# Top-k attention and a low-rank mixer: masking of the tails moves from VectorE to ScalarE and GpSimd

## The chip, the cores and the metric

One core of a Trainium2 chip runs the whole kernel. The metric is the device time of one execution in microseconds (us). Names of the engines in the profile: PE is TensorE (PEld its weight loads), DVE is VectorE, ACT is ScalarE, POOL is GpSimd, SP is SyncE, which issues most of the DMA transfers. The engines run side by side; each takes its own instructions strictly in the order in which the program issues them, and waits at an instruction until its inputs are ready and its output buffer is free.

## What is computed

Two blocks follow each other, all in float32:

```python
# attention: q, k, v are (8 batches, 8 heads, 576 rows, 64)
scores = scale * np.matmul(q, k.transpose(0, 1, 3, 2))
kth = np.partition(scores, -32, axis=-1)[..., -32:-32 + 1]
scores = np.where(scores >= kth, scores, -1000000000.0)
attn = softmax(scores)                    # exp, then divided by (sum + 1e-9)
x = np.matmul(attn, v)                    # then heads side by side: (8, 576, 512)

# mixer: U (576, 32), V (32, 576), w_ch1 (512, 2048), w_ch2 (2048, 512)
h = x.transpose(0, 2, 1) @ U @ V
u = x + h.transpose(0, 2, 1)
out = u + np.maximum(u @ w_ch1, 0.0) @ w_ch2
```

For every row of scores only the 32 largest of 576 take part in the softmax. U, V and the two large weights come as float64 and are converted on the chip, in pieces, while the attention of the first batches runs.

## The kernel before

**Pairs and steps.** The attention is done for pairs of heads: pair g (0 to 31) holds two heads of one batch, four pairs to a batch. A pair takes five steps. Steps t = 0 to 3 treat 128 rows of each head: two chunks of 128 x 576 scores, chunk 0 for the first head, chunk 1 for the second. Step t = 4 is the tail: the last 64 rows of both heads, stacked into one chunk of 128 x 576. Steps are numbered n = 5 g + t.

**One step** (`front`). `scores` has put the chunks into SBUF (Ssb, copied from PSUM by ACT one step ahead). VectorE finds the 8 largest of each row (L339, `first`), then three times replaces the 8 found by a very low number (L351) and finds the next 8 (L355). The last of the 32 is the row's threshold. A chunk is then masked and its exponential taken in one of three ways:

- *early*: ACT takes the exponential of the whole chunk soon after the first maximum is known (L348, `weigh`, L312); after the last maximum VectorE multiplies it by "score is at least the threshold" and sums the row (L361, `scalar_tensor_tensor`; the sum needs a short second instruction).
- *pooled* (chunk 1 of full steps): POOL computes a very low number where the score lies below the threshold (L358) and adds it to the scores (L359); ACT then takes the exponential with the row's sum.
- *gap* (chunk 0 of the steps for which `eased` is true): ACT forms `least`, the threshold times 2^96 (L375), and Relu of 2^96 times how far the score lies below the threshold (L376); POOL subtracts that from the scores (L377); ACT then takes the exponential with the sum (L381).

Before the change, full steps of the first two batches (g < 8) take *pooled* and *gap*. The exception is step 3 of pair 3, the last full step of the first batch: both its chunks are *early*. All tails are *early*. From the third batch on, full steps take *early* and *pooled*.

**After the mask.** `turns` transposes the exponentials on TensorE (L397, L402) and ACT copies them out of PSUM (PT, L398, L403); `values` multiplies them with v (L421, L431, L434); `mixed` scales by the reciprocal of the row sums (`inverse`, L409 and L410 on VectorE; L460 on POOL), and adds the low-rank part (L466 to L488). When all four pairs of a batch are through, its MLP (`mlp`, matmuls L503 and L522, ACT's Relu L515, POOL's add L538) becomes a list of fillers, which `fill` takes up in portions between the instructions of the next batch's attention. So the first batch has no MLP work beside it, and from then on there is always some.

**Order.** The order of each engine is written out by hand in the loop over n: `front(n)`, `turns` and the others are generators, and each `next(...)` issues one piece. `here` is the front of this step, `last` that of the step before. If the step before was eased, its gap piece is issued at the start of this step (in the batches after the first too) and its exponentials after that; in the first batch the exponentials come after the second `next(here)`. Steps 19 and 20 (the tail of pair 3 and the first step of pair 4), where the first batch ends, have a branch of their own (L612 to L643). `next_params` issues the float64 conversion: ACT L165 to L168, VectorE L175, POOL L176 and L178.

**Buffers.** Ssb and E have three buffers each, the transposes' PSUM tile two, PT two.

Of the kernel before, what the change touches and what calls it, by code (L numbers as in the profile page):

```python
# [11 lines left out]
AF = mybir.ActivationFunctionType  # L12
ALU = mybir.AluOpType

TOPK = 32
NEG = -3.0e38
# [4 lines left out]
WIDEN = 2.0**96  # L21
# [5 lines left out]
def kernel(  # L27
# [28 lines left out]
    nc = tc.nc  # L56
# [6 lines left out]
    NT, TAIL = 4, 64  # L63
# [3 lines left out]
    NPAIR = H // 2  # L67
# [243 lines left out]

        nc.scalar.activation(E, chunk, AF.Exp, bias=nmax, scale=SCALE, accum_out=total)  # L312

    def eased(g, t):


        return g < 2 * NPAIR and t < NT and (g, t) != (NPAIR - 1, NT - 1)

    def front(g, t):

        if t == 0:
            dens[g] = small.tile([P, 2 * NT + 1], F32, tag="den", name="den", bufs=3)
        chunks, den = S2s.pop((g, t)), dens[g]
        n = len(chunks)
        E2 = attn.tile([P, 2 * S], F32, tag="E", name="E", bufs=3)
        Es = [E2[:, c * S : (c + 1) * S] for c in range(n)]  # L330
        sums = [den[:, 2 * t + c : 2 * t + c + 1] for c in range(n)]
        probs[g, t] = E2
        curs, ms = list(chunks), [None] * n
        first = small.tile([P, 2, 8], F32, tag="first", name="first", bufs=3)
        nmax = small.tile([P, 2], F32, tag="nmax", name="nmax", bufs=4)
        order = (1, 0) if n == 2 else (0,)
        for c in order:
            ms[c] = first[:, c]
            nc.vector.max(ms[c], curs[c])  # L339
        yield  # L340
        ease = eased(g, t)
        pooled = n == 2 and (g, t) != (NPAIR - 1, NT - 1)
        early = range(0 if ease else 1 if pooled else n)
        for i in range(1, TOPK // 8):
            if i == 1:
                nc.scalar.mul(nmax[:, 0:n], first[:, 0:n, 0], -SCALE)
                for c in early:
                    weigh(chunks[c], Es[c], nmax[:, c : c + 1])  # L348
            for c in order:
                nxt = attn.tile([P, S], F32, tag="rr", name="rr", bufs=3)  # L350
                nc.vector.match_replace(nxt, ms[c], curs[c], NEG)  # L351
                curs[c] = nxt
            for c in order:
                ms[c] = small.tile([P, 8], F32, tag="m8", name="m8", bufs=8)
                nc.vector.max(ms[c], curs[c])  # L355
            yield
        if pooled:
            nc.gpsimd.tensor_scalar(Es[1], chunks[1], ms[1][:, 7:8], NEG, ALU.is_lt, ALU.mult)  # L358
            nc.gpsimd.tensor_tensor(chunks[1], chunks[1], Es[1], ALU.add)  # L359
        for c in early:  # L360
            nc.vector.scalar_tensor_tensor(  # L361
                out=Es[c],
                in0=chunks[c],
                scalar=ms[c][:, 7:8],
                in1=Es[c],
                op0=ALU.is_ge,
                op1=ALU.mult,
                accum_out=sums[c],
            )
        if t == NT:  # L370
            del qkTs[g]
        yield
        if ease:
            least = small.tile([P, 1], F32, tag="least", name="least", bufs=3)
            nc.scalar.mul(least, ms[0][:, 7:8], WIDEN)  # L375
            nc.scalar.activation(Es[0], chunks[0], AF.Relu, bias=least, scale=-WIDEN)  # L376
            nc.gpsimd.tensor_tensor(chunks[0], chunks[0], Es[0], ALU.subtract)  # L377
            yield
        for c in order:
            if c not in early:  # L380
                weigh(chunks[c], Es[c], nmax[:, c : c + 1], sums[c])  # L381
        if t == NT and g != NPAIR - 1:
            nc.scalar.activation(den, den, AF.Identity, bias=eps)
        yield
# [27 lines left out]
    def values(g, t):  # L412

        PT = PTs.pop((g, t))
        va, vd, vt = (a[g % NV] for a in (vas, vds, vts))
        O = ps_t.tile([P, P], F32, tag="tp", name="O")
        if t == NT:
            den, x = dens[g], xs[g % 2]
            inverse(g, 2 * NT if g == NPAIR - 1 else 0, 2 * NT + 1)
            for j in range(NT + 1):  # L420
                nc.tensor.matmul(  # L421
                    O,
                    lhsT=PT[:, j],
                    rhs=va[:, :, j, :] if j < NT else vt,
                    start=(j == 0),
                    stop=(j == NT),
                )
            for h in range(2):
                nc.scalar.mul(x[half(h), NT, half(h)], O[half(h), half(h)], den[half(h), 2 * NT :])
            return  # L430
        nc.tensor.matmul(O, lhsT=vd, rhs=PT[:, 2 * NT], start=True, stop=False)  # L431
        for j in range(NT):
            for h in range(2):
                nc.tensor.matmul(  # L434
                    O[half(h)],
                    lhsT=va[:, h, j, :],
                    rhs=PT[:, NT * h + j],
                    start=False,
                    stop=(j == NT - 1),
                )  # L440
        if t == 0:
            XTs[g] = attn.tile([P, MAIN], F32, tag="XT", name="XT")
        nc.scalar.copy(XTs[g][:, cols(t)], O)  # L443
# [152 lines left out]
    t = 0  # L596
# [5 lines left out]
    for n in range(STEPS + 2):  # L602
        g, t = divmod(n, CH)
        if n < STEPS:
            if t == 0 and g + 1 < NP:
                load(g + 1)
            if t == 1 and g + 1 < NP:
                ready = prep(g + 1)
            fronts[n] = front(g, t)
            next(fronts[n])  # L610
        here, last = fronts.get(n, iter(())), fronts.pop(n - 1, iter(()))
        if n >= ALONE - 1 and n <= ALONE:  # L612

            if n < ALONE:
                values(*divmod(n - 3, CH))
                list(turning)
                scores(*divmod(n + 1, CH))
                values(*divmod(n - 2, CH))
                next(here)
            list(turns(*divmod(n - 1, CH)))  # L620
            values(*divmod(n - 1, CH))
            if n < ALONE:
                inverse(g, 0, 2 * NT)
                next(here)
                mixing.append(mixed(g, 1))
                fill()
                next(here)
                next(here)
                continue
            fill()  # L630
            scores(*divmod(n + 1, CH))
            next(here)
            while mixing:
                fill()
            next_params(1)
            fill()
            next(last, None)
            next(here)
            fill()
            next(here)  # L640
            next(here)
            fill()
            continue  # L643
        ease = eased(*divmod(n - 1, CH))
        if n < ALONE:
            if ease:
                next(last, None)
            scores(*divmod(n + 1, CH))
            if n >= 3:
                values(*divmod(n - 3, CH))  # L650
                if (n - 3) % CH == NT:
                    mixing.append(mixed((n - 3) // CH, 3))
            list(turning)
            fill()
            next(here)
            if t < NT:
                next_params(1)
            fill()
            next(ready, None)
            next(here)  # L660
            next(last, None)
            fill()
            next(here)
            if t in (0, 1):
                next_params(1)
            next(here)
            fill()
            if n >= 1:
                turning = turns(*divmod(n - 1, CH))
            continue  # L670
        if ease:
            next(last, None)
        fill()
        next(turning, None)
        fill()
        next(turning, None)
        fill()
        next(ready, None)
        fill()
        if ease:  # L680
            next(last, None)
        if n - 2 >= ALONE:
            values(*divmod(n - 2, CH))
        if n + 1 < STEPS:
            scores(*divmod(n + 1, CH))
        next(here, None)
        next_params(1)
        if n - 2 >= ALONE and (n - 2) % CH == NT:
            mixing.append(mixed((n - 2) // CH, 4))
        fill()  # L690
        next(here, None)
        fill()
        if n <= STEPS:
            turning = turns(*divmod(n - 1, CH))
        next(turning, None)
        fill()
        next(here, None)
        next(last, None)
        if t in (1, 3):
            next_params(1)  # L700
        next(here, None)
        fill()
# [33 lines left out]
```

## Time and profile before

| what | us |
|---|---|
| median of five runs | 1850.42 |
| the five runs | 1848.48, 1848.49, 1850.42, 1850.67, 1850.97 |
| the profiled execution, time | 1848.48 |
| its span in the trace | 1846.7 |
| VectorE L361, 130 instructions, mean of one with its read | 0.89 |
| ACT L376, 31 instructions, mean | 0.776 |
| POOL L377, 31 instructions, median | 1.412 |
| POOL L358 and L359, mean | 2.236 and 1.409 |

The profile is of one execution. It gives for every instruction its start and length and, where its engine stood idle before it, which instruction ended the wait. A line such as "PE tp L397 <- ACT E L312" means that TensorE's transpose of line 397 waited for the exponential of line 312. The granted clock is the share of TensorE's full clock that it was given.

### The profile page before, as it was taken

The numbers are of one execution on the slowest core, as the hardware profiler recorded it, in microseconds if no ns is written. First come the engines' busy times: TensorE is split into PE (matmuls) and PEld (weight loads), VectorE is DVE, ScalarE is ACT, GpSimd is POOL, SyncE is SP. The second block draws the span as 40 slices with busy tenths as digits, with TensorE's granted clock in tenths as the row PEclk, the third lists the DMA queues.
The fourth block names the chain that finished last, engine by engine and source line by source line (L and its number), as shares of the span: only waits on it lengthen the run. The fifth ranks groups of instructions, "written<-read, shape, count | busy, mean of one in ns | idle before, by whom it ended". The sixth has DMA issues, their size and how long they took to land.

```text
span 1846.7 us, 29134 instructions
## 1 busy us (share of the span) xinstructions
PE 1740.1 (94%) x10528; PEld 1317.0 (71%) x10528; DVE 1575.9 (85%) x3224; ACT 1008.2 (55%) x2494; POOL 672.6 (36%) x463
## 2 busy tenths in 40 slices
PE   4666889999999999999999999999999999999999
PEld 2444556787777877787777877788777877778677
DVE  7999988998999999998999999999999999996000
ACT  5777777665645555555555555555555556454110
POOL 4677577443333323423223332323224333332000
PEclk7678899999999999999999999999999999999999
DMA  4232221101001010111000010110001010000000
GB/s 109 77 85 84 69 77 47 31 21 32 20 22 28 15 27 20 31 25 31 15 25 20 23 30 21 30 24 24 17 19 31 21 32 19 10 8 7 6 15 12
DMA packets 127295, 58.22 MB, mean 32 GB/s; under 512 B 89904, under 2 KB 124976, under 8 KB 127152
## 3 DMA queue, kind: packets, MB, share of 16 engines
q1 hardware_dynamic: 126096, 56.10, 11.4%
q8 instruction: 84, 1.38, 0.3%
q14 instruction: 59, 0.48, 0.1%
q10 hardware_dynamic: 1056, 0.26, 0.1%
HBM read 46.89 MB, written 9.44 MB: 31 GB/s over the span
## 4 chain that ended last, share of the span: by engine, by line
PE 84%; DVE 9%; POOL 3%; ACT 2%; issue 1%; DMA 0%; SPq 0%; POOLq 0%; DVEq 0%; ACTq 0%
PE mm L503 26%; PE mm L522 26%; PE sc L294 7%; PE O L434 6%; PE tp L397 6%; DVE rr L351 4%; DVE m L355 3%; PE sc L281 2%; PE O L421 2%; PE up L478 2%; PE O L431 1%; DVE first L339 1%; PE tp L266 1%; PE tp L550 1%; PE up L480 1%
## 5 line engine op out<-in xcount | busy, mean ns | idle before, releaser
L355 DVE MAX8 m<-rr 128x8 f32<-128x576 f32 x864 | 614.7, 748 | 5.5
L522 PE MATMUL mm<-hT,w 128*128 128x256 f32 (+1 forms) x2048 | 563.8, 411 | 0.0
L503 PE MATMUL mm<-uT,w 128*128 128x256 f32 (+1 forms) x2048 | 557.0, 410 | 1.6 <-ACT hT L515 1.6
L358 POOL TENSOR_SCALAR E<-Ssb,m 128x576 f32<-128x576 f32 x127 | 284.0, 2236 | 584.4 <-DVE m L355 398.3
L503 PEld LDWEIGHTS mm<-uT,w 128*128 128x128 f32 x2048 | 363.5, 190 | 107.9 <-issue 27.6
L522 PEld LDWEIGHTS mm<-hT,w 128*128 128x128 f32 x2048 | 361.4, 191 | 98.2 <-issue 23.3
L351 DVE MATCH_REPLACE8 rr<-m,rr 128x576 f32<-128x576 f32 x576 | 427.6, 742 | 0.0
L398 ACT COPY PT<-tp 128x512 f32<-128x512 f32 x288 | 168.4, 587 | 128.8 <-PE tp L397 127.9
L312 ACT ACTIVATE E<-Ssb,nmax 128x576 f32<-128x576 f32 x288 | 222.8, 776 | 24.4 <-POOL Ssb L359 14.2
L351 DVE MATCH_REPLACE8 rr<-first,Ssb 128x576 f32<-128x576 f32 x288 | 211.7, 741 | 0.0
L397 PE MATMUL tp<-ident,E 128*128 128x128 f32 x1152 | 179.2, 280 | 31.7 <-ACT E L312 13.4
L339 DVE MAX8 first<-Ssb 128x8 f32<-128x576 f32 x288 | 205.0, 748 | 1.5 <-ACT Ssb L307 1.5
L397 PEld LDWEIGHTS tp<-ident,E 128*128 128x128 f32 x1152 | 142.6, 144 | 82.4 <-ACT E L312 22.9
L361 DVE SCALAR_TENSOR_TENSOR E<-Ssb,m,E 128x576 f32<-128x576 f32 x130 | 115.7, 890 | 90.4 <-ACT E L312 78.0
L359 POOL TENSOR_TENSOR Ssb<-Ssb,E 128x576 f32<-128x576 f32 x127 | 179.0, 1409 | 10.6
L294 PE MATMUL sc<-qkT 64*128 64x288 f32 x1024 | 169.3, 451 | 11.7 <-ACT Ssb L305 7.7
L515 ACT ACTIVATE hT<-mm 128x320 f32<-128x320 f32 (+1 forms) x256 | 104.2, 407 | 119.1 <-PE mm L503 118.7
L434 PE MATMUL O<-PT,va 128*64 128x128 f32 x2048 | 143.0, 283 | 0.0
L443 ACT COPY XT<-O 128x128 f32<-128x128 f32 x128 | 34.2, 267 | 182.2 <-PE O L434 182.2
L294 PEld LDWEIGHTS sc<-qkT 64*128 64x128 f32 x1024 | 92.3, 196 | 50.2 <-issue 16.5
L538 POOL TENSOR_TENSOR oT<-oT,uT 128x320 f32<-128x320 f32 (+1 forms) x56 | 44.6, 796 | 224.5 <-ACT oT L537 224.5
L434 PEld LDWEIGHTS O<-PT,va 128*64 128x64 f32 x2048 | 111.7, 139 | 15.9 <-issue 0.9
(80 smaller groups left out, 1533.4 us busy)
## 6 DMA issues: line engine op xcount, KB each, us to landing
raw<-in_moe_w_ch_dram SPq DMA_DIRECT2D x32, 512.0 KB, 3.7
va<-in_v_dram SPq DMA_DIRECT2D x64, 128.0 KB, 2.4
out_dram<-ob SPq DMA_DIRECT2D x64, 128.0 KB, 1.9
ld_q<-in_q_dram SPq DMA_DIRECT2D x63, 128.0 KB, 2.7
ld_k<-in_k_dram SPq DMA_DIRECT2D x63, 128.0 KB, 2.7
ld_ends<-in_q_dram SPq DMA_DIRECT2D x32, 32.0 KB, 2.1
ld_ends<-in_k_dram SPq DMA_DIRECT2D x32, 32.0 KB, 2.1
vd<-in_v_dram SPq DMA_DIRECT2D x64, 16.0 KB, 2.0
```

What stands on the lines that cost most here:

```text
L294: nc.tensor.matmul(sc[:, h, 0:HALF], lhsT=qkT[half(h), 0, cols(t)], rhs=qkT[half(h), 1, i * HALF : (i + 1) * HALF], start=True, stop=True,)
L312: nc.scalar.activation(E, chunk, AF.Exp, bias=nmax, scale=SCALE, accum_out=total)
L339: nc.vector.max(ms[c], curs[c])
L351: nc.vector.match_replace(nxt, ms[c], curs[c], NEG)
L355: nc.vector.max(ms[c], curs[c])
L358: nc.gpsimd.tensor_scalar(Es[1], chunks[1], ms[1][:, 7:8], NEG, ALU.is_lt, ALU.mult)
L359: nc.gpsimd.tensor_tensor(chunks[1], chunks[1], Es[1], ALU.add)
L397: nc.tensor.transpose(tp[:, j, :], E2[:, a : a + P], ident)
L398: nc.scalar.copy(PT[:, NT * h : NT * h + NT], tp)
L434: nc.tensor.matmul(O[half(h)], lhsT=va[:, h, j, :], rhs=PT[:, NT * h + j], start=False, stop=(j == NT - 1),)
L503: nc.tensor.matmul(ph[:, 0:w], lhsT=w1[:, cc, f * P : (f + 1) * P], rhs=uT[:, cc, lo:hi], start=(cc == 0), stop=(cc == NC - 1),)
L522: nc.tensor.matmul(po[:, 0:w], lhsT=w2[:, f, c * P : (c + 1) * P], rhs=hTs[f][:, 0:w], start=(f == 0), stop=(f == NF - 1),)
```

## The change

A new function `ways` says for each step which chunks are *early*, *pooled* and *gap*, and `eased` follows from it. Two groups of chunks change their way:

- the tails of the first two batches, except that of pair 3 (pairs 0, 1, 2, 4, 5, 6, 7): from *early* to *gap*;
- chunk 1 of step 3 of pair 3: from *early* to *gap*.

Since `eased` is now true for these steps, their gap piece and their exponential are issued in the step after. In the branch of step 19 two `next(last)` are added for the second group, and the `next(here)` that issues the tail's first round (ACT's nmax and exponential among it) now comes before the copies of the next scores. A step's small addition of 1e-9 to the sums (L383) follows the tail's exponential.

```diff
+    def ways(g, t):
+        if g < 2 * NPAIR and (g, t) != (NPAIR - 1, NT):
+            if (g, t) == (NPAIR - 1, NT - 1):
+                return (0,), (), (1,)
+            return (), (1,) if t < NT else (), (0,)
+        return (0,), (1,) if t < NT else (), ()
+
     def eased(g, t):
-        return g < 2 * NPAIR and t < NT and (g, t) != (NPAIR - 1, NT - 1)
+        return bool(ways(g, t)[2])
...
-        ease = eased(g, t)
-        pooled = n == 2 and (g, t) != (NPAIR - 1, NT - 1)
-        early = range(0 if ease else 1 if pooled else n)
+        early, pooled, gaps = ways(g, t)
...
-        if pooled:
-            nc.gpsimd.tensor_scalar(Es[1], chunks[1], ms[1][:, 7:8], NEG, ALU.is_lt, ALU.mult)
-            nc.gpsimd.tensor_tensor(chunks[1], chunks[1], Es[1], ALU.add)
+        for c in pooled:
+            nc.gpsimd.tensor_scalar(Es[c], chunks[c], ms[c][:, 7:8], NEG, ALU.is_lt, ALU.mult)
+            nc.gpsimd.tensor_tensor(chunks[c], chunks[c], Es[c], ALU.add)
...
-        if ease:
+        for c in gaps:
             least = small.tile([P, 1], F32, tag="least", name="least", bufs=3)
-            nc.scalar.mul(least, ms[0][:, 7:8], WIDEN)
-            nc.scalar.activation(Es[0], chunks[0], AF.Relu, bias=least, scale=-WIDEN)
-            nc.gpsimd.tensor_tensor(chunks[0], chunks[0], Es[0], ALU.subtract)
+            nc.scalar.mul(least, ms[c][:, 7:8], WIDEN)
+            nc.scalar.activation(Es[c], chunks[c], AF.Relu, bias=least, scale=-WIDEN)
+            nc.gpsimd.tensor_tensor(chunks[c], chunks[c], Es[c], ALU.subtract)
             yield
...
             if n < ALONE:
+                next(last)
                 values(*divmod(n - 3, CH))
                 list(turning)
+                next(here)
+                next(last)
                 scores(*divmod(n + 1, CH))
                 values(*divmod(n - 2, CH))
-                next(here)
             list(turns(*divmod(n - 1, CH)))
```

## The prediction

> **What bounds the kernel now.** I read the page's engine sums and forty slices first, then a table of busy time by stage, then the waits of VectorE and TensorE, and last the timeline at three places: a tail, the border of the two first batches, and the first tail of batch 1.
>
> The page, sums and slices (a digit is a slice of 46.2 us):
>
> ```profile
> PE 1740.1 (94%) x10528; PEld 1317.0 (71%) x10528; DVE 1575.9 (85%) x3224; ACT 1008.2 (55%) x2494; POOL 672.6 (36%) x463
> PE   4666889999999999999999999999999999999999
> DVE  7999988998999999998999999999999999996000
> ```
>
> The sums say TensorE. The slices say that this is an average over two kernels: up to some 200 us VectorE is full and TensorE half idle. The table by stage (length; busy PE, PEld, DVE, ACT, POOL; granted clock; DMA):
>
> ```profile
> 11.00:218.40 207.40, 127.19 (x792) 84.47 (x789) 204.21 (x421) 148.23 (x355) 136.33 (x100) 0.75 0.29 82
> 218.40:318.00 99.60, 89.54 (x523) 62.47 (x522) 89.06 (x178) 75.93 (x179) 73.55 (x51) 1.00 0.23 70
> 318.00:1691.00 1373.00, 1367.59 (x8527) 1047.91 (x8526) 1277.24 (x2612) 756.83 (x1894) 457.29 (x293) 1.00 0.09 23
> ```
>
> Until 218.4, where the first MLP matmul starts, VectorE is busy 204.21 of 207.40 us: it sets the time. From 318 on TensorE is busy 1367.59 of 1373.00: nothing saved on VectorE counts there, and the end is the moment of 318 plus fixed matmul work. Between lies a mixed stage: TensorE idles 10.06 us of 99.60, in waits that lead back to VectorE, through POOL and ACT. So the question is by how much the change moves the moment of 318. TensorE's order of instructions is the same in both kernels.
>
> The waits up to 320 us (who waits, on whom: us in total, times, the longest), first VectorE's, then TensorE's from 205 us on:
>
> ```profile
> DVE E L361 <- ACT E L312: 11.1, 3, 5.9
> ...
> PE tp L397 <- ACT E L312: 3.3, 2, 2.0
> PE pT L466 <- POOL x L460: 1.7, 1, 1.7
> ```
>
> VectorE's only wait of weight in this stretch is L361's own; TensorE's longest are for exponentials and for POOL.
>
> The timeline of VectorE at the tail of pair 0 (start, length), at the tail of pair 4, and of TensorE at 317.6:
>
> ```profile
> 58.04 0.76 DVE L355 MAX8 m<-rr 128x8 f32<-128x576 f32 x1
> 58.94 0.82 DVE L361 SCALAR_TENSOR_TENSOR E<-Ssb,m,E 128x576 f32<-128x576 f32 x1
> 59.68 1.42 DVE L339 MAX8 first<-Ssb 128x8 f32<-128x576 f32 x2
> ...
> 258.40 0.76 DVE L355 MAX8 m<-rr 128x8 f32<-128x576 f32 x1
> 264.05 0.82 DVE L361 SCALAR_TENSOR_TENSOR E<-Ssb,m,E 128x576 f32<-128x576 f32 x1 [4.89 <-ACT E L312]
> 264.80 1.42 DVE L339 MAX8 first<-Ssb 128x8 f32<-128x576 f32 x2
> ...
> 317.61 0.88 PE L397 MATMUL tp<-ident,E 128*128 128x128 f32 x4 [1.95 <-ACT E L312]
> 318.28 3.29 PE L522 MATMUL mm<-hT,w 128*128 128x320 f32 x6
> ```
>
> The masking multiply (L361) sits between a tail's last maximum and the next pair's first one. At pair 4 it also makes VectorE stand 4.89 us for an exponential.
>
> **The change, part by part.**
>
> *Tails of pairs 0, 1, 2 (batch 0).* VectorE loses one L361 each. From the start of the last maximum to the next pair's first maximum are 59.68 - 58.04 = 1.64 us; two maxima back to back start 1.41 - 0.74 = 0.67 apart. So 0.97 us each (107.26 to 108.90 and 156.48 to 158.12 give the same), 3 x 0.97 = 2.91. VectorE is full here, the next scores lie ready 4 us before (their last copy ends at 153.85 for the maximum at 158.12), so all of it counts. Instead ACT gets least and Relu (L375 0.20, L376 0.78), an accumulator read (0.19), and the exponential later; POOL a subtraction (L377, 1.41). All this falls in step t = 0 of the next pair, where ACT has an idle stretch of 2.3 to 3.5 us before its next least and POOL one of 6.6 before the parameter join at 64.28, 113.49, 162.71. The transposes that read the result come a step later. Cost 0. If that cover were gone, the scores copies behind the Relu would slip by 1 us; their reader is 8 us away. No DMA or queue of SP is moved.
>
> *Second head of pair 3's step 3.* One of two L361 goes: 202.40 - 201.66 = 0.74 saved. But its sum now comes from ACT, and VectorE's den add (L409, 204.79) follows it in the middle of the tail's four maxima. Walk ACT, in the clock of before: the early exponential of this head is gone from the pair at 196.63, so the queue runs 0.68 ahead and ends the pair's earlier exponentials at 201.1 instead of 201.8. Least and Relu to 202.05; POOL, idle from 198.9 on, subtracts to 203.5. TensorE's transposes start 0.68 sooner (201.92 to 201.24); their three copies end at 203.95; then nmax (0.2), the tail's exponential (0.7), the head's exponential and sum (1.0): 205.85. So L409 starts at 205.9, not 204.79: +1.1 where -0.74 was to be had. Behind it stand the tail's remaining two rounds; the 0.29 that VectorE waits at 208.61 goes (that exponential is now early), and the first maximum of pair 4 starts at 210.18 instead of 209.35: **+0.83**. TensorE, meanwhile, gains: the copies of PT at 208.48 waited behind the tail's exponential, which now lies before them, so its chain to the first MLP matmul ends about 1.0 earlier. The wait is bounded by 0 (VectorE -0.74) and by the longest that VectorE now waits for L312, 5.9 at 319.80 (then about +5.2). I take +0.83 since it is added up from rows within 15 us of the place.
>
> *Tails of pairs 4 to 7 (batch 1).* At pair 4 VectorE no longer stands for the exponential; it waits for the scores instead, whose last copy (262.82, 0.28) ends at 263.10: 264.80 - 263.10 = **1.70** saved. Does TensorE follow? Its waits from 262 to 299 are 0.76 at 266.41 (a PT copy, which comes 0.7 earlier as ACT's exponential at 263.24 leaves the queue), 1.73 at 286.16 (POOL's x, three steps from VectorE) and 0.51: 2.5 to 3.0 of slack for 1.7, so yes. From 286.47 to 316.7 POOL is nearly full and leads to 317.61; its start hangs on VectorE's shift (285.74), its restart at 299.36 on TensorE's matmul before 298.85, and both move alike. The bounds: 0 if TensorE or ACT keeps the old pace, 1.70. I take 1.70. Tails 5, 6 and 7 lie at 318 and later: TensorE's stage, 0 (if TensorE no longer covered them, another 0.97 saved each). Their 1.41 of POOL falls into its idle 12.59 and 14.34 us (before 330.07 and 380.51).
>
> Sum: -2.91 + 0.83 - 1.70 = **-3.78 us** at 318, and so at the end. Profiled execution: span 1846.7, time 1848.48, which gives 1844.7. It is the lowest of the five (two at 1848.48 and 1848.49, three from 1850.42 to 1850.97), 1.94 below the median; on the median, 1850.42 - 3.78 = **1846.6**.
>
> *The clock.* After the 1.95 us idle before 317.61 four transposes took 0.88 (at 309.64: 0.60) and six matmuls 3.29 (at 308.02: 1.78): 1.8 us lost, with 0.58 granted from 318 to 322. A stretch of that kind may go or another come as idle stretches shift: 1.8 either way, kept for the range. The Trainium skill, TensorE: Matmul & The Clock Gate, HAM oscillation, warns only of idle gaps above some 3.4 us. The trace lowers the clock after less. By the page nothing would be at stake here and the sum stays -3.78; the row decides for the range.
>
> **Rivals.**
>
> *More arrives (0.25).* The stretch at 318 disappears, or ACT reaches the head's sum before VectorE needs it (-0.74 instead of +0.83). For it: TensorE reaches the border 1.0 earlier than VectorE's path asks. Against: ACT's queue is full from 196.1 to 201.9. It gives -5.4 by the border alone, -7.1 with 1.8 of clock: 1845.0 to 1843.3.
>
> *Only the first tails count (0.20).* The 1.70 stays on VectorE as idle, and a half-rate stretch comes: -2.08, then -0.3 with 1.8 of clock: 1848.3 to 1850.1. For it: ACT is busy 75.93 of 99.60 and gains work per tail. Against: the 2.5 us of TensorE's own waits.
>
> *Slower (0.10).* The exponentials of batch 1's tails come too late for TensorE, which has no slack there. A tail's E was ready at its L361; now it needs Relu, POOL and the exponential in the next step, and ACT's exponential, waiting for POOL, holds the scores copies behind it. Price per tail: the waits of these transposes for L312 are 1.95 at 317.61 and 3.3 at the longest. Four times 1.95 is 7.8, less 3.78: +4.0, 1854.4. It decides from 1.9 us of lateness per tail ((3.78 + 3.7) / 4). Against: for pair 4 Relu fits at 266, POOL idles from 263.5 to 269.45, the exponential ends by 269.3, and the transposes start at 272.43: 3 us of margin.
>
> **How the numbers follow.** My forecast has 0.45, with a range of its own of 1845.4 to 1847.8 (1.2 either way, one exponential with its read more or less in ACT's queue at the border); the rest is as named. 0.2% is 3.7 us, about what a measurement of this kernel can tell from no change, and my sum lies on that edge: 0.27 of the 0.45 and the 0.25 above make faster 0.52; 0.18 and 0.20 make same 0.38; slower is 0.10. The range reaches from the best case, 1843.2, past the second rival's worst to the far bound of the border's wait (-2.91 + 5.2 - 1.70 = +0.6), 1851.0.
>
> **What would show.** The row of L361 (L366 after) has 122 instructions, not 130; those of L376 and L377 (L381, L382) 39, not 31. Right if: the first maximum of pair 1 starts near 58.7 and that of pair 3 near 155.2; L409 (L414 after) of pair 3 waits some 1.9 us for ACT, around 203.0; the first maximum of pair 4 starts near 207.3 and of pair 5 near 261.0; the first MLP matmul near 214.5; TensorE's stage without idle begins near 314. Wrong if VectorE's wait at the border passes 4 us, if transposes of E (L397, L402 after) wait for exponentials in steps t = 0 of pairs 5 to 8, or if more half-rate stretches follow 215 us than the one.

## The result and the profile after

| what | before | after |
|---|---|---|
| median, us | 1849.99 (44 runs, 1848.48 to 1851.00) | 1846.38 (24 runs, 1845.15 to 1848.34) |
| ratio after to before | | 0.9982, 95% interval 0.9976 to 0.9987 |
| profiled execution, time | 1848.48 | 1845.56 |
| its span | 1846.7 | 1843.4 |

The change takes about 3.6 us, 0.18%. The interval leaves no change out, and it lies across the bound of 0.2% that the prediction named. The forecast of 1846.6 is met within 0.3 us, but that is a sum of several errors that partly cancel, as the traces show; so close a hit is in part luck. The time of an execution is longer than its span, in the profiled one of before by 1.8 us and in that of after by 2.2; over the runs of after this excess lies between 1.75 and 2.98 us, and where it comes from is open. So effects below 1 us are read from the traces, not from the times.

The page of after, sums and slices (a digit is 46.1 us):

```profile
PE 1734.4 (94%) x10528; PEld 1311.8 (71%) x10528; DVE 1570.5 (85%) x3208; ACT 1015.2 (55%) x2518; POOL 684.4 (37%) x471
PE   4656889999999999999999999999999999999999
DVE  7999998899999999998999999999999999996000
```

VectorE has 16 instructions fewer (eight multiplies with their reads), ACT 24 more, POOL 8 more. The form of the kernel is the same: first VectorE, then TensorE. The table by stage (length; busy PE, PEld, DVE, ACT, POOL; granted clock; DMA):

```profile
11.00:214.50 203.50, 121.56 (x794) 79.89 (x791) 199.54 (x409) 151.99 (x368) 141.99 (x104) 0.79 0.29 83
214.50:314.00 99.50, 89.08 (x517) 61.44 (x515) 90.36 (x180) 76.08 (x180) 74.91 (x53) 1.00 0.24 71
314.00:1691.00 1377.00, 1371.45 (x8545) 1051.03 (x8546) 1275.18 (x2606) 762.02 (x1910) 462.08 (x296) 1.00 0.09 23
```

The first stage is 3.9 us shorter, the mixed stage as long as it was, and from 314 on TensorE is the bound as it was from 318. So the question stays by how much the moment of 318 moved. The waits up to 320 us, VectorE's, then TensorE's from 205 us on (who waits, on whom: us in total, times, the longest):

```profile
DVE first L346 <- ACT Ssb L307: 9.9, 3, 5.0
DVE den L414 <- ACT E L312: 1.3, 1, 1.3
...
PE tp L402 <- ACT E L312: 4.8, 3, 1.9
PE pT L471 <- POOL x L465: 1.2, 1, 1.2
```

Before, VectorE's 11.1 us were waits of the multiply for exponentials. Now it waits for the next scores instead (L346), and once, new, for the sum of the head that was moved at the border (L414).

The timeline of VectorE, then of TensorE at 314 (start, length, what ended the idle time before):

```profile
58.15 0.76 DVE L360 MAX8 m<-rr 128x8 f32<-128x576 f32 x1
58.82 1.40 DVE L346 MAX8 first<-Ssb 128x8 f32<-128x576 f32 x2
...
202.61 0.17 DVE L414 TENSOR_SCALAR den<-den 128x8 f32<-128x8 f32 x1 [1.29 <-ACT E L312]
207.01 1.42 DVE L346 MAX8 first<-Ssb 128x8 f32<-128x576 f32 x2
260.76 1.42 DVE L346 MAX8 first<-Ssb 128x8 f32<-128x576 f32 x2 [3.98 <-ACT Ssb L307]
264.87 1.00 DVE L175 TENSOR_SCALAR w<-w 128x512 uint32<-128x512 uint32 x1
...
314.12 0.66 PE L402 MATMUL tp<-ident,E 128*128 128x128 f32 x4 [1.93 <-ACT E L312]
314.61 2.99 PE L527 MATMUL mm<-hT,w 128*128 128x320 f32 x6
```

At pair 0's tail the next first maximum follows the last one after 0.67 us, as two maxima do. Reading the same rows in both traces gives the shift of after against before:

| start of VectorE's first maximum of | before | after | shift | what lies between |
|---|---|---|---|---|
| pair 1, step 0 | 59.68 | 58.82 | -0.86 | first tail; all of after starts 0.11 later |
| pair 2, step 0 | 108.90 | 107.07 | -1.83 | second tail |
| pair 3, step 0 | 158.12 | 155.31 | -2.81 | third tail |
| pair 3, step 3 | 189.75 | 186.92 | -2.83 | |
| pair 4, step 0 | 209.35 | 207.01 | -2.34 | the border: +0.49 |
| pair 5, step 0 | 264.80 | 260.76 | -4.04 | tail of pair 4: -1.70 |
| pair 5, step 1 | 275.05 | 271.60 | -3.45 | +0.59 |
| pair 5, step 4, and TensorE from 286 to 314 | | | -3.47 | |
| the end of the span | 1846.7 | 1843.4 | -3.3 | 0.18 lost at 738 us |

### The profile page after: what moved, and what is told of

Read it like the earlier page. It is cut to its first block, busy times and chain, and to the rows that moved or that the text cites. A ratio compares the mean times of both kernels' runs of the same rounds, so it can differ in the third digit from the quotient of the medians.

```text
span 1843.4 us, 29145 instructions
## 1 busy us (share of the span) xinstructions
PE 1734.4 (94%) x10528; PEld 1311.8 (71%) x10528; DVE 1570.5 (85%) x3208; ACT 1015.2 (55%) x2518; POOL 684.4 (37%) x471
## 4 chain that ended last, share of the span: by engine, by line
PE 83%; DVE 10%; POOL 3%; ACT 2%; issue 1%; DMA 0%; SPq 0%; POOLq 0%; DVEq 0%; ACTq 0%
PE mm L508 26%; PE mm L527 26%; PE sc L294 7%; PE O L439 6%; PE tp L402 6%; DVE rr L356 4%; DVE m L360 3%; PE sc L281 2%; PE O L426 2%; PE up L483 2%; PE O L436 1%; DVE first L346 1%; PE tp L266 1%; PE tp L555 1%; PE up L485 1%
## 5 line engine op out<-in xcount | busy, mean ns | idle before, releaser
L363 POOL TENSOR_SCALAR E<-Ssb,m 128x576 f32<-128x576 f32 x127 | 283.9, 2235 | 562.9 <-DVE m L360 402.0
L346 DVE MAX8 first<-Ssb 128x8 f32<-128x576 f32 x288 | 205.1, 748 | 19.1 <-ACT Ssb L307 19.1
L294 PE MATMUL sc<-qkT 64*128 64x288 f32 x1024 | 167.5, 447 | 12.6 <-ACT Ssb L305 8.5
L366 DVE SCALAR_TENSOR_TENSOR E<-Ssb,m,E 128x576 f32<-128x576 f32 x122 | 109.3, 896 | 73.6 <-ACT E L312 60.8
L294 PEld LDWEIGHTS sc<-qkT 64*128 64x128 f32 x1024 | 91.3, 193 | 50.4 <-issue 16.2
```

Source lines behind the costliest of these rows:

```text
L294: nc.tensor.matmul(sc[:, h, 0:HALF], lhsT=qkT[half(h), 0, cols(t)], rhs=qkT[half(h), 1, i * HALF : (i + 1) * HALF], start=True, stop=True,)
L363: nc.gpsimd.tensor_scalar(Es[c], chunks[c], ms[c][:, 7:8], NEG, ALU.is_lt, ALU.mult)
```

## The experiments

Two things were open: what each part is worth, and whether the border and the return of 0.59 are parts of the change's price that can be avoided. My theory was the sum of the prediction, with the two deviations of the table; the rivals were that the head at the border costs more than it shows, and that the granted clock, not the change, makes the border's wait. All medians are us; "before" beside each was run on the same chip at the same time. It was 1850.47 beside e5 to e8 and 1848.94, on the same chip a quarter of an hour later, beside e9 to e12, so the medians of these two sets are not compared as they stand.

**The parts.** The first four kernels take the change apart (before: 1850.36). Each edits `ways`; without the head the branch of step 19 stands as before.

```diff
# e1_no_border: all the tails, without the head of pair 3
+        if (g, t) == (NPAIR - 1, NT - 1):
+            return (0, 1), (), ()
+        if g < 2 * NPAIR and (t < NT or g in (0, 1, 2, 4, 5, 6, 7)):
# e2_border_only: the head as in after, no tail
+            return (0,), (), (1,)
+        if g < 2 * NPAIR and (t < NT or g in ()):
# e3_tails_first, e4_tails_second: as e1, with
+        if g < 2 * NPAIR and (t < NT or g in (0, 1, 2)):
+        if g < 2 * NPAIR and (t < NT or g in (4, 5, 6, 7)):
```

> The change without the second head of pair 3 (chunk 1 of its step 3 stays early, the branch of step 19 as before); all seven tails are masked by the gap. Theory: at the border the first maximum of pair 4 lost 0.49 us of what the tails had won (its shift falls from -2.83 at pair 3's step 3 to -2.34), because VectorE's den add waits 1.29 us for ACT where one 0.74 us multiply is saved; that wait is the gate for the exponentials of batch 1, so without it the gain is 2.94 + 1.1 = 4.0 us, some 0.5 us faster than the change: first maximum of pair 4 at -2.9, TensorE at -4.0 from 285 us on, time near 1846.0. Rival (the head is worth having because TensorE reaches the MLP 1.4 us earlier with it, -4.36 against -2.94): without it the time is 0.7 to 1.4 us above the change's, 1847.1 to 1847.8.

> Only the second head of pair 3 changes its way, all tails stay early. Theory: VectorE saves 0.74 us and waits 1.3 to 1.9 us for the head's sum; the first maximum of pair 4 starts 0.5 to 1.1 us later than before, TensorE's first MLP matmul 0.7 to 1.4 us earlier, and the time is 0.5 to 1.1 us longer than before's. Rival (TensorE's earlier start counts): 0.7 to 1.4 us shorter.

> Only the tails of pairs 0, 1 and 2 are masked by the gap. Theory: VectorE sets the time up to the border, 0.97 us saved per tail arrive whole: first maximum of pair 4 at -2.9 us, and as the stage from 218 to 318 us hangs on VectorE through POOL and ACT, the end at -2.9 too: 1847.1. Rival (the mixed stage has its own pace, by POOL's joins or TensorE's own work): part of it is given back before 318 us, the end at 0 to -1.5.

> Only the tails of pairs 4 to 7 are masked by the gap. Theory: pair 4's tail saves 1.70 us on VectorE (no wait for the exponential) and loses 0.59 us again when the parameter shift L175 of the next step runs beside the added subtraction of POOL (1.00 us instead of 0.41): the end at -1.1 us, 1848.9; pairs 5 to 7 give nothing, as TensorE is full there. Rivals: the loss is not from this overlap and the end is at -1.7; or TensorE does not follow VectorE here and the end is at 0.

| kernel | median (runs, range) | ratio, 95% interval |
|---|---|---|
| e1_no_border | 1845.26 (8, 1843.63 to 1846.11) | 0.9974, 0.9963 to 0.9984 |
| e2_border_only | 1850.73 (11, 1849.62 to 1851.68) | 1.0003, 0.9994 to 1.0012 |
| e3_tails_first | 1846.66 (11, 1845.75 to 1848.20) | 0.9982, 0.9973 to 0.9991 |
| e4_tails_second | 1849.09 (11, 1847.80 to 1850.22) | 0.9996, 0.9986 to 1.0005 |

By medians the head alone gives +0.4, the first three tails -3.7, those of the second batch -1.3. Only e1 and e3 are told from no change. The first tails carry the change; the second batch's add less than the 1.70 that VectorE gains there, and the profile of e4 shows why: pair 5 step 0 gains 1.65 against pair 4, and 0.58 of it is gone at step 1, as in after. Another 0.29 goes at step 2, where the shift takes 1.09 us (0.79 in after). The head's own price is not settled by these medians: e1 is 1.1 below after, and the intervals of the two overlap. In the profiled executions TensorE in e1 is 0.34 ahead of after at 313 us.

At the border the traces were a surprise. e1 and e3 have the same code up to there, yet from pair 3 step 3 to pair 4 step 0 e1 loses 0.05 us and e3 loses 2.42. (e4, with the same code there, loses 0.89.) VectorE in e3 (with, as in before, a masking multiply in the tail, L363 there), and in e2, where it is the sum's addition (L411 there):

```profile
208.25 0.82 DVE L363 SCALAR_TENSOR_TENSOR E<-Ssb,m,E 128x576 f32<-128x576 f32 x1 [2.67 <-ACT E L312]
```

```profile
207.17 0.17 DVE L411 TENSOR_SCALAR den<-den 128x8 f32<-128x8 f32 x1 [2.65 <-ACT E L312]
```

So waits of 2.7 us come with the head and without it. What differs is TensorE's clock. Windows of TensorE in e3 (length, busy PE, granted clock, DMA share, GB/s):

```profile
194.00:198.00 4.00, 1.32 (x10) 1.00 0.08 17
198.00:202.00 4.00, 3.35 (x22) 0.55 0.39 130
202.00:206.00 4.00, 4.00 (x19) 0.60 0.02 4
206.00:210.00 4.00, 2.92 (x29) 1.00 0.00 0
```

TensorE idles 3.33 us before 198.65, then runs at 0.55 and 0.60 for eight. ACT, which takes its work in order, stands behind it. ACT in e3, at the tail's exponential:

```profile
204.91 0.64 ACT L305 COPY Ssb<-sc 128x576 f32<-128x576 f32 x1 [0.87 <-PE sc L294]
...
207.04 0.27 ACT L445 COPY XT<-O 128x128 f32<-128x128 f32 x1 [0.74 <-PE O L436]
207.20 0.21 ACT L348 ACTIVATE nmax<-first 128x1 f32<-128x1 f32 x1
207.44 0.78 ACT L312 ACTIVATE E<-Ssb,nmax 128x576 f32<-128x576 f32 x1
```

The exponential for which VectorE waits starts at 207.44 since the copies of the scores and of the values' product ahead of it wait for TensorE. A slow TensorE thus costs time in a stage where VectorE is the bound.

**The clock at the border.** Twelve more 128 x 128 matmuls per step in steps 15 to 18, of the identity with itself into a PSUM tile that nobody reads, keep TensorE from idling there; three follow each of a step's four `fill()`. e7 is e1 with them, e9 before, e10 after. Nothing of the computation is left out.

```diff
+    def warm(k):
+        if ALONE - 5 <= n < ALONE:
+            idle = ps_m.tile([P, C], F32, tag="mm", name="idle")
+            for _ in range(k):
+                nc.tensor.matmul(idle[:, 0:P], lhsT=ident, rhs=ident, start=True, stop=True)
...
             fill()
+            warm(3)
```

> The change without the head of pair 3, as in the first of these runs, and with 12 matmuls of 128 x 128 on an unused bank in each of the steps 15 to 18, whose results nobody reads. Theory (at the border VectorE waits for the tail's exponential as long as TensorE's half clock delays the copies in front of it; 0.29 us in one execution, 2.67 in another): with fewer idle stretches the clock from 186 to 206 us is near 1.0, the tail's multiply of pair 3 waits under 0.3 us in the profile, and the slow executions vanish: the highest time falls from 1846.1 towards 1845.2, the median by 0.3 to 0.6 us. Rival (the added matmuls stand before the real ones in TensorE's order, or the clock isn't what delays them): the median is the same or 0.5 to 1 us longer.

> The kernel before, with the 12 unread matmuls in each of the steps 15 to 18. Theory (half clock at the border is what spreads the executions over 2.5 us and costs the median part of it): clock near 1.0 from 186 to 206 us, the tail's multiply of pair 3 waits 0.3 us or less, time at or under the lowest of before, 1847.0 to 1848.3. Rival (the matmuls helped in the kernel without the head of pair 3 for another reason, such as an idle stretch at 314 us that went): the time stays near 1850.

> The change, with the same unread matmuls. Theory: at full clock the wait before L414 is 1.3 us as in the change's profile, not the 3.1 us seen at half clock, and the head of pair 3 costs the 0.49 us by which VectorE falls back at the border: 0.5 us above the kernel without it (1842.96), 1843.5, and 3.5 us below before with the same matmuls. Rival (the head costs by itself, whatever the clock): 1.1 us above 1842.96 as without the matmuls (1846.38 against 1845.26), 1844.1 or more.

| kernel | median (runs, range) | before beside it | ratio, 95% interval |
|---|---|---|---|
| e7_warm | 1842.96 (5, 1842.74 to 1844.66) | 1850.47 | 0.9962, 0.9950 to 0.9975 |
| e9_before_warm | 1847.24 (11, 1847.08 to 1848.62) | 1848.94 | 0.9989, 0.9980 to 0.9997 |
| e10_after_warm | 1845.03 (7, 1842.92 to 1845.55) | 1848.94 | 0.9972, 0.9961 to 0.9984 |

TensorE in e7, the same columns:

```profile
198.00:202.00 4.00, 3.59 (x33) 1.00 0.38 120
202.00:206.00 4.00, 2.92 (x29) 1.00 0.02 4
```

With full clock the tail's multiply in e7 waits for nothing, and the border costs -0.11. It is the same in e9 (-0.11) and in e11 (-0.10, below), against +0.05 to +2.42 in e1, e4 and e3 with the same code at a reduced clock. That the clock makes the border's wait is shown by this.

The time is another matter. By the medians the unread matmuls make before itself 1.7 faster, and ten of its eleven runs lie within 0.4 us, where those of before spread over 2.5. But in the profiled executions only 0.15 of it comes at the border, where the profiled one of before had waited just 0.29: the first maximum of pair 4 starts at 209.20 in e9 and at 209.35 in before. TensorE gains 1.70 at 317 us, over 110 us after the last unread matmul, since there the half-rate stretch of before does not follow the same idle time; 0.48 of that is lost again by 349 us. TensorE in e9, first a row of the timeline, then a window:

```profile
317.44 0.66 PE L397 MATMUL tp<-ident,E 128*128 128x128 f32 x4 [1.94 <-ACT E L312]
316.00:320.00 4.00, 2.56 (x15) 1.00 0.01 2
```

So the rival of e9's expectation, an idle stretch at 314 us that went, is what this pair of traces shows. Executions of before with a slower border would have more to gain there, but none was profiled. e7 against e1 is the same: at 313 us they are 0.05 apart, and the 1.7 between their spans comes at this stretch. In e10 the wait at L414 stays, though shorter:

```profile
202.28 0.17 DVE L414 TENSOR_SCALAR den<-den 128x8 f32<-128x8 f32 x1 [0.94 <-ACT E L312]
```

The border there costs +0.16. So at full clock the head costs 0.16 + 0.11 = some 0.3 us against masking it early, not more (0.49 + 0.11 = 0.6 in after itself). That e10 is 2 us behind e7 has another cause, below.

**The sum's addition later.** The wait at L414 stands in the middle of the tail because `inverse` is issued ahead of a round of maxima. e5 issues it behind that round.

```diff
-                inverse(g, 0, 2 * NT)
                 next(here)
+                inverse(g, 0, 2 * NT)
```

> The change, with VectorE's den add and reciprocal of pair 3 issued one round of maxima later in step 19, so that the sum from ACT is there when VectorE comes to it. Theory (that wait is what the head of pair 3 costs): the 1.29 us before L414 go, the first maximum of pair 4 comes 1.2 us earlier than in the change (near 205.8), and the time is some 1 us below the change's, 1845.4 and below. Rival (ACT is the gate at the border, and the next maxima or the next scores wait for it instead): the first maximum of pair 4 stays at 207.0, the time at 1846.4.

e5: 1844.74 (6 runs, 1842.65 to 1845.55), ratio 0.9970 (0.9958 to 0.9982). Its profiled execution fell on a border at half clock (0.50 and 0.78), and still the wait was short:

```profile
204.42 0.17 DVE L414 TENSOR_SCALAR den<-den 128x8 f32<-128x8 f32 x1 [1.00 <-ACT E L312]
```

The border cost 0.20 there, against 2.27 in e6 (below) at nearly the same clock, 0.50 and 0.75, with the addition at its old place: at half clock the move is worth 2 us. Against after, whose border ran at full clock, the expected 1.2 us did not come: the first maximum of pair 4 started at 207.16, as the rival had it (207.01 in after; 0.44 of the 207.16 is a later start of the whole execution). That the median is 1.6 below after's has another cause, below.

**The return of 0.59.** In after, the conversion's shift (L175) at 264.87 took 1.00 us; the one before was 0.41 at its counterpart. POOL beside it, in after:

```profile
264.18 1.41 POOL L382 TENSOR_TENSOR Ssb<-Ssb,E 128x576 f32<-128x576 f32 x1 [3.03 <-ACT E L381]
265.94 1.29 POOL L176 TENSOR_TENSOR w<-w,raw 128x512 uint32<-128x512 uint32 x1 [0.36 <-DVE w L175]
```

and before's shift:

```profile
268.90 0.41 DVE L175 TENSOR_SCALAR w<-w 128x512 uint32<-128x512 uint32 x1
```

POOL's subtraction, which the change adds there, ends at 265.59, and VectorE's shift, started in its midst, ends only at 265.87. e6 issues that step's conversion one round later, so that the two do not meet.

```diff
         next(here, None)
-        next_params(1)
+        if not (n == ALONE + CH):
+            next_params(1)
...
         next(here, None)
+        if n == ALONE + CH:
+            next_params(1)
```

> The change, with the parameter conversion of step 25 (the first of pair 5) issued one round of maxima later, so that VectorE's shift L175 no longer meets POOL's added subtraction. Theory (the two block each other): the shift takes 0.41 us instead of 1.00, the second step of pair 5 starts at -4.0 instead of -3.45 us against before, TensorE follows, and the time is 0.5 to 0.6 us below the change's, 1845.8. Rival (the loss is in something else of the step): L175 keeps 0.8 to 1.0 us or the step its pace, the time 1846.4.

e6: 1845.58 (10 runs, 1843.91 to 1847.58), ratio 0.9976 (0.9967 to 0.9985). VectorE in e6, at the border and in step 25:

```profile
204.68 0.17 DVE L414 TENSOR_SCALAR den<-den 128x8 f32<-128x8 f32 x1 [3.07 <-ACT E L312]
...
269.83 0.41 DVE L175 TENSOR_SCALAR w<-w 128x512 uint32<-128x512 uint32 x1
...
277.23 1.10 DVE L175 TENSOR_SCALAR w<-w 128x512 uint32<-128x512 uint32 x1
```

The shift is 0.41 again, and pair 5 step 1 keeps the gain of step 0 (-1.98 at both). But the next shift takes 1.10 instead of 0.79, as it does (1.08 and 1.09) in e2 and e4 without this edit: 0.3 of the 0.59 is lost there. The overlap is shown as the cause; what it is worth is 0.3. The border of this execution fell on half clock (0.50 and 0.75), and there the head's wait of 3.07 costs 2.27.

**Together.** e8 is after with the edits of e5 and e6; e12 is e8 with the unread matmuls; e11 is e7 with e6's edit.

> The change with both moves, the reciprocal of pair 3 and the conversion of step 25 one round later. Theory: 1.2 and 0.6 us add up on VectorE, the time is 1.5 us below the change's, near 1844.8, which beats the change and the change without the head of pair 3 (1845.3). Rival (TensorE or POOL is the next bound between 218 and 314 us): under 0.8 us below the change's.

> The change without the head of pair 3, with the unread matmuls, and with the conversion of step 25 one round later. Theory: L175 takes 0.41 us there, which is 0.6 us less on VectorE and 0.3 to 0.6 at the end: 1842.4 to 1842.7. Rival (TensorE is the bound by then): no change, 1843.0.

> The change with the reciprocal of pair 3 and the conversion of step 25 one round later, and with the unread matmuls. Theory: at full clock the sum from ACT is there when VectorE comes to it, the head of pair 3 then saves its 0.74 us, and with 0.3 to 0.6 us from the conversion this is the fastest: 1841.7 to 1842.3, first maximum of pair 4 at -3.6 us against before. Rival (ACT is the gate at the border at any clock): no faster than the kernel without the head and with the matmuls, 1842.4 to 1843.0.

| kernel | median (runs, range) | before beside it | ratio, 95% interval |
|---|---|---|---|
| e8_both | 1843.49 (5, 1842.24 to 1845.15) | 1850.47 | 0.9964, 0.9951 to 0.9976 |
| e11_no_border_warm_join | 1844.25 (5, 1842.61 to 1844.44) | 1848.94 | 0.9968, 0.9956 to 0.9981 |
| e12_both_warm | 1843.44 (5, 1841.76 to 1843.66) | 1848.94 | 0.9963, 0.9950 to 0.9975 |

In e12 the wait at L414 is gone at last, and the border gains 0.88:

```profile
202.79 0.15 DVE L414 TENSOR_SCALAR den<-den 128x8 f32<-128x8 f32 x1
204.77 0.82 DVE L366 SCALAR_TENSOR_TENSOR E<-Ssb,m,E 128x576 f32<-128x576 f32 x1
```

Against the border without the head at full clock (-0.11 in e7) that is 0.77. So the head does save its multiply (0.74) where the clock is full and its sum is read a round later.

**Two groups of runs.** e10, e11 and e12 missed what e7 had reached. Their runs fall into two groups: e10 near 1843.0 (2) and 1844.9 to 1845.6 (5), e11 1842.61 (1) and 1844.06 to 1844.44 (4), e12 1841.8 to 1842.1 (2) and 1843.4 to 1843.7 (3). e7 has four low runs and one 1.7 above them. The profiled executions tell them apart at 312 to 320 us. TensorE in e7, a low run, and in e10, a high one:

```profile
316.00:320.00 4.00, 4.00 (x34) 1.00 0.01 4
```

```profile
312.00:316.00 4.00, 2.17 (x8) 0.81 0.00 0
316.00:320.00 4.00, 4.00 (x15) 0.77 0.00 0
```

This is the half-rate stretch that the prediction named and put at 1.8. It explains more than the warm kernels. The table gives, for the profiled executions, how far TensorE is ahead (-) of before when it starts the scores (L294) that begin at 313.14 and at 325.45 us in before, just ahead of the stretch and just behind it; before's own stretch is slow.

| kernel | at 313 us | at 325 us | clock after the idle time |
|---|---|---|---|
| after | -3.47 | -3.50 | reduced |
| e1_no_border | -3.81 | -3.80 | reduced |
| e5_inverse_later | -3.26 | -4.97 | full |
| e6_join_later | -1.69 | -1.70 | reduced |
| e7_warm | -3.86 | -5.55 | full |
| e8_both | -3.68 | -5.38 | full |
| e9_before_warm | -0.16 | -1.86 | full |
| e10_after_warm | -3.78 | -3.78 | reduced |
| e11_no_border_warm_join | -4.08 | -4.09 | reduced |
| e12_both_warm | -5.22 | -5.22 | reduced |

The edits act up to 313 us; the 1.7 behind it comes with and without the unread matmuls, and no edit is shown to bring it or keep it away. All five profiled executions of the warm kernels agree: e7 and e9 low at full clock, e10, e11 and e12 high at a reduced one. Within equal groups the numbers line up: e11 is 0.3 below e7 (the overlap's 0.3) in both groups, 1842.61 to 1842.96 and 1844.3 to 1844.66; e12 is 0.6 to 0.8 below e11 (the head, with its sum read later); and e10 against e9 is -4.2 in the low group (-3.6 by the traces at 313 us). The groups have one to five runs, so these differences are supported by the traces' shifts and not by intervals of their own.

By the medians e7, e8 and e12 beat both kernels; their intervals against before lie below that of after (0.9976 to 0.9987), e8's just touching it. But of the lead of e7 and e8 over after in the spans (2.2 and 1.9 us) 1.7 is the stretch; up to 313 us they lead by 0.4 and 0.2, and e5 trails by 0.2. So the 1.5 us that e8's two moves were to bring did not come in its profiled execution, whose border ran at 0.62 from 198 to 202 us and cost 0.43. Only e12 leads clearly at the same level as after, with a slow stretch in both: by 1.75 at 313 us and 1.7 in the span.

## Why the prediction was right, and where it was not

*Tails of pairs 0, 1, 2, -2.91.* Right. They gave 2.92 in the trace of after (2.81 with the 0.11 of a later start) and 3.7 by e3's median, which mixes in the clock at the border and at 314.

*Second head at the border, +0.83.* Right in mechanism: the wait is at L414, where the prediction put it, ended by ACT's exponential. The term was mis-sized: 1.85 us of wait were added up and 1.29 came, and the border cost 0.49. What the walk along ACT's queue could not know is that it took one clock out of several. The wait is 0.94 and 1.29 at full clock (e10, after), 2.65 and 3.07 at a reduced one (e2: 0.72 and 0.50 from 198 to 206 us; e6: 0.50 and 0.75). The walk was made in the trace of before, which ran at 0.59 in that place. That TensorE's chain would end about 1.0 earlier was right in sign and more: the first MLP matmul moved from 218.4 to 214.1, by 4.36 on the rows, which is 1.5 more than VectorE's shift before the border. It counted for nothing: TensorE gave it back at 237, waiting 1.55 us for an exponential.

*Tail of pair 4, -1.70.* The step that failed. The 1.70 arrives to the hundredth: VectorE now waits 3.98 us for the scores. But a third of it goes back 4 us later, where the tail's new subtraction on POOL meets the shift of step 25. I had laid POOL's work into POOL's idle time, and did not ask what VectorE runs beside it; there the cover was wrong, as the subtraction costs VectorE, not POOL. e4 shows the same return without the rest of the change, and e6, e8, e11 and e12 take the meeting away.

The Trainium skill, SBUF — State Buffer, section "Who interferes with whom", says that VectorE and GpSimd share a pair of ports which one instruction holds for its whole length, and names `tensor_scalar` among VectorE's operations that can claim it. The traces agree: the shift of 0.41 us alone took 1.00 and ended 0.28 us after POOL's subtraction. In before 13 of the 14 shifts that met a two-input operation of POOL took 0.57 to 1.57 us and ended 0.28 or 0.29 us after it; the one that met only its last 0.03 us took 0.41. Beside POOL's one-input comparison alone (L358) eight of nine took 0.40 to 0.41, the ninth 0.58; the section does not make that difference.

*Tails 5 to 7, 0.* Right: from 286 us on the shift holds at -3.47 to -3.50, up to 738 us, and TensorE is busy 1371.45 of 1377.00.

*The sum.* -3.78 was predicted for the moment of 318 and -3.47 came: the border 0.34 better, the overlap 0.59 worse, the later start 0.11 worse. The span shows 0.18 less, lost at one transpose at 738 us; why is open. The six kernels that move both the head and all seven tails lose 0.2 between 725 and 778 us, the others nothing.

*The clock.* The stretch behind the 1.9 us of idle before 314 stayed in the profiled execution: six matmuls took 2.99 (before 3.29, alone 1.78). The price of 1.8 was right: it is 1.7 between the traces with and without it. What was too narrow is its place: I looked for it only at 318, and such stretches also lie at the border, where they cost 2.27 in e6 and 2.42 in e3. Runs of before and after spread over some 3 us; in e9, with the border at full clock and, in its profiled execution, no slow stretch at 317, ten of eleven lie within 0.4.

The Trainium skill, TensorE: Matmul & The Clock Gate, HAM oscillation, warns of idle gaps above 3.4 us. The traces lower the clock after less: after 2.69 us in e6 (granted 0.50 from 198 to 202) and after 1.93 to 1.97 near 314; and not each time, since after has the same 2.69 us at 1.00, and e7 the same 1.94. The page also says, under "What's actually happening", that the window is free-running, so that the moment of a change varies; that would fit gaps with and without a slow stretch, but no run here shows the window.

*The rivals.* That more arrives did not come in after; e12 shows its condition, the sum read a round later and a full clock (0.88 gained at the border). That only the first tails count is refuted by -1.70 and the -1.11 that stay of it. The slower one: TensorE's waits for exponentials from 314 on come to the one of 1.93 that was there before, so tails 5 to 7 are not late.

## What to carry to other kernels

Work moved to an idle engine is free only if it does not slow what the busy engine runs beside it (here a shift of 0.41 us became 1.00): look in the timeline at what the bound engine executes during the new instructions, not only at whether the new engine is idle. Where the bound engine waits for a copy that another engine makes from a slow third one, TensorE's clock counts even at half load: here the same code cost between -0.1 and 2.4 us at the border. A few unread matmuls in its gaps kept the clock up there; the 1.7 us by which before got faster with them lies elsewhere in the traces, and that they brought it is not shown. With a run-to-run spread that has two levels, compare profiled executions of the same level, or their shifts just ahead of the place that splits the levels, before putting a difference of 1 or 2 us down to an edit.

## What the runs showed of the hardware that was not expected

- The same code at the border lost 0.05 us in e1 and 2.42 in e3; the granted clock of the two was 0.64 and 0.93 against 0.55 and 0.60 from 198 to 206 us.
- A 128 x 512 shift on VectorE took between 0.40 and 1.57 us in before, by what POOL ran beside it; where it met a two-input operation of POOL it ended 0.28 or 0.29 us after it, in 13 of 14 cases.
- Nearly identical idle gaps of TensorE (1.93 to 1.97 us, ending between 312 and 320) were followed by full clock in e2, e5, e7, e8 and e9 and by a reduced one in the other nine profiled executions. What decides it stays open; the order of the work cannot be tied to it here.
